# Transposes as pairs of 64-row tiles, narrower Gram products, SwiGLU on two slices at once, narrowing in four raw buffers, and a new instruction order

## The chip, the cores and the metric

The kernel runs on one core of one Trainium2 chip. The metric is the device time of one execution in microseconds (us); the time before is the median of three runs. One more execution was taken with the hardware profiler; its rows are the source of every duration in this document. Engines are called as in the profile: PE is the matrix engine (TensorE), PEld its weight loads, DVE the vector engine, ACT the scalar engine, POOL and SP the two engines that mostly issue transfers here.

## The reference

An RWKV-7 recurrence is followed by a SwiGLU feed-forward block. Shapes are batch 4, heads 8, sequence 768, head dimension 40; the outputs of the 8 heads side by side are the 320 features of 3072 tokens.

```python
for t in range(S):
    y[:, :, t] = np.einsum('bhd,bhde->bhe', rt, state)
    Sa = np.einsum('bhde,bhe->bhd', state, at)
    state_decay = state * wt[:, :, None, :] - np.einsum('bhd,bhe->bhde', Sa, bt)
    state = state_decay + np.einsum('bhd,bhe->bhde', vt, kt)
...
xn = x / rms * rms_g
g = xn @ w_gate
silu = g * (1.0 / (1.0 + np.exp(-g)))
val = xn @ w_val
return (silu * val @ w_out).astype(np.float32)
```

The weights `w_gate` and `w_val` are 320 x 1536 and `w_out` is 1536 x 320. They arrive as 64-bit floats: the kernel reads them as pairs of 32-bit words and makes 32-bit floats of them ("narrowing"). All matrix products are in 32-bit floats.

## The kernel before, in words

The sequence is cut into 24 chunks of 32 tokens; 32 sequences (batch x head) are worked on together. For a chunk, `front` loads the inputs token by token, turns them so that features lie on partitions, builds the decayed products of keys and values with the gates level by level (levels 1, 2, 4, 8, 16; these are the Gram products), and writes the triangular matrix LT of the chunk. `inverse` (for the first chunks `early_inverse`) inverts it on DVE. `main` makes the outputs of the chunk and the next state, turns the outputs back to tokens, normalizes them and turns them again into `xg`, the input of the feed-forward block. `front` runs two chunks ahead of `main`.

`feed` (L939) does the feed-forward block for a group of two chunks, 256 tokens. The 1536 hidden columns are 12 slices of 128, taken in six pairs. For each slice the weights (480 KB, one tile `wf`) are loaded from a copy `sW` in HBM; two products on 64 rows each (the last 64 features of gate and value; below "the 64-row products") and four on 128 rows give gate and value in PSUM, ACT makes `sg` = silu(gate), DVE makes `hT` = value * sg, and two products of 128 x 320 add the slice to the output `po`. Before group 0, and between its pairs, `narrow` (L973) makes the 24 halves of `sW` from the 64-bit weights, in the same rotating five `wf` tiles that `feed` uses.

A transpose on PE takes the data as the loaded operand and streams the identity through it. `turned` (L630) does eight of them, one for each pair of heads: the data of 128 rows is loaded with up to 104 columns, and 128 columns of identity are streamed; for K and ST it is 104 rows and 104 columns of identity. A chunk has such batches for wan, kbn, VU, K and ST, and one for rn in every second chunk; besides there are four transposes of y and three of x, 128 x 128 each. Transposes appear under L489, all products under L486.

A 32-bit product is two passes in the trace, so the profile counts two records for it; a transpose is one record. Small products use a part of the array each: the Gram products load 40 rows and 64 columns and stream 56 columns, so four of them have places of their own (two groups of rows, two of columns).

The order of all engines is written out. Each call of a helper adds a piece to `Plan`; `Plan.issue` takes the pieces in the order of the string `ORDER`, a number for each, and assigns one of three PSUM pairs ("rooms") by the string `PAIRS`. A "-" in `ORDER` puts a product of the identity with itself on PE (L1015, `plan.warm`), whose result is not used. Every engine works off its pieces in this order and waits at the first whose inputs are not there. `ORDER` has 6028 pieces and 151 of these warm products.

Of the kernel before, what the change touches and what calls it, by code (L numbers as in the profile page):

```python
# [17 lines left out]
P = 128  # L18
# [3 lines left out]
WB = 5  # L22
LEAD = 2
# [10 lines left out]
85 83 84 76 58 78 86 74 73 59 60 75 5 89 61 88 77 4 43 6 201 7 87 334 90 44 8 214 213 53 62 9 - - - - - - - - 93 18 10  # L34
567 335 557 11 12 13 79 14 15 94 566 80 210 16 95 558 108 17 200 - - - 97 96 19 20 100 21 2 22 101 23 98 25 568 202 24
26 107 112 57 - - - - - 102 106 111 124 27 209 122 392 103 109 52 119 113 104 54 578 569 577 155 199 125 110 105 204
120 - - - - - - 114 203 118 117 121 559 211 598 589 562 46 131 129 132 45 560 212 597 563 588 561 123 115 136 586 384
133 134 - - - - - 126 130 116 47 564 3 145 216 394 383 135 336 128 137 48 144 143 141 91 587 219 142 51 570 127 1005
565 146 138 337 55 573 579 281 393 220 582 608 571 390 234 239 607 572 583 580 380 574 251 222 38 221 609 575 581 42 -
- - - - - - - 223 82 226 339 64 379 227 338 39 81 139 224 263 149 576 238 153 56 249 247 590 206 584 228 382 237 591  # L40
593 272 40 233 232 381 154 0 593 32 139 390 204 228 591 388 234 249 247 - - 324 235 35 31 27 244 229 146 147 259 281
245 258 149 34 325 594 36 33 270 155 243 62 605 584 598 230 - 239 40 214 599 601 242 628 64 49 91 627 602 30 626 1135
600 28 48 257 603 29 241 68 150 255 65 0 1347 194 0 194 84 173 0 - - - 182 540 200 0 184 1 186 542 540 0 506 0 457 469
849 199 455 242 111 97 110 112 96 51 61 439 460 458 122 50 243 0 0 255 242 0 709 104 470 242 120 246 259 708 57 247
458 456 0 257 718 256 470 242 0 716 265 487 486 0 268 0 0 265 101 473 0 262 277 0 273 0 236 0 260 0 269 0 242 461 - -
- - - - - 237 0 240 0 278 242 252 0 242 252 0 90 0 0 98 99 246 0 0 230 440 0 230 94 93 457 440 231 - - - - - - - - -
240 441 244 0 44 0 468 440 255 0 450 468 269 469 0 257 214 439 238 213 203 0 257 203 93 449 92 0 0 234 - - - - - - - -
245 437 0 250 262 0 464 246 247 436 260 245 446 258 259 469 244 - - 255 471 465 468 470 466 0 269 215 255 478 466 93
94 264 95 96 266 97 0 97 470 1 2 98 99 0 0 96 467 97 469 98 468 251 265 99 470 100 471 101 441 102 103 258 104 105 260
106 - - - - - - - - - - - 0 106 107 471 108 0 108 502 503 472 0 108 109 110 111 0 0 0 0 0 - - 13 0 16 562 572 146 571  # L50
561 147 14 142 143 374 15 13 355 - - - 25 386 358 0 358 386 388 16 25 387 389 390 70 79 17 391 28 191 147 355 356 80
148 149 359 0 68 28 2 29 149 0 149 34 150 29 151 187 24 25 31 152 33 153 188 391 393 32 154 35 390 392 358 0 0 152 40
187 153 27 154 155 156 33 157 158 159 160 161 34 162 36 163 164 37 165 41 391 38 42 392 39 394 561 166 395 393 552 0
42 559 549 548 395 209 0 549 560 42 165 210 43 44 211 427 428 395 - - - 565 166 45 167 557 168 0 565 566 168 739 0 522
693 534 526 124 - - 0 526 124 139 0 535 681 682 579 0 535 545 547 140 536 138 141 0 547 545 555 543 578 0 558 520 567
- - - - - - 518 378 0 696 378 380 381 695 518 120 685 526 - - - - - - 522 686 379 527 382 136 530 383 554 529 121 - -
141 540 523 565 539 537 142 538 524 - - - - 145 525 148 534 149 152 154 551 535 147 555 - - 157 146 550 536 150 155
# [3 lines left out]
478 595 568 - - 35 830 594 567 820 38 36 - 476 37 571 366 570 0 605 356 433 434 435 436 120 437 0 317 318 319 320 441  # L61
321 322 323 355 456 324 458 459 442 4 357 325 457 326 327 443 328 0 443 328 329 330 331 357 0 35 0 330 2 37 450 359 3
36 358 331 332 357 333 356 0 462 330 461 464 448 331 332 468 364 447 463 31 467 476 458 333 365 334 335 0 425 439 441
302 426 436 0 6 439 2 0 435 332 2 436 443 444 0 448 332 442 334 443 333 340 449 0 32 297 329 342 330 - 3 338 33 341
334 0 332 331 0 332 293 441 0 438 0 436 293 333 336 295 337 309 438 338 1 375 342 310 365 374 515 27 292 0 362 26 28
44 339 29 34 292 27 32 338 0 646 29 34 336 32 0 439 64 315 647 646 339 440 441 63 340 0 287 413 312 313 623 12 414 314
415 315 416 608 624 32 417 480 418 625 419 420 421 316 626 638 33 0 312 417 625 418 - - - - 476 313 601 602 600 610
812 419 420 421 822 258 422 423 0 313 810 423 625 637 2 0 819 2 0 254 473 420 421 645 310 422 0 - - - - - 310 422 3
313 33 0 28 626 307 419 639 627 420 637 308 0 637 20 635 420 647 21 421 23 422 613 648 819 38 22 809 423 39 659 24 611
3 612 36 818 424 651 808 621 425 25 660 426 - 616 249 427 0 427 3 25 58 57 428 28 47 0 428 429 28 430 3 431 0 26 25  # L70
614 484 31 27 617 627 0 458 216 400 590 600 401 0 12 582 32 401 583 25 0 397 579 21 - - - - - - - - - 588 29 28 30 591
22 453 428 398 605 23 0 591 23 429 602 24 609 0 24 397 588 602 1 604 398 429 430 2 399 427 0 584 - - - - - - - - - - -
- - - 4 397 0 25 397 4 0 393 394 21 23 27 28 395 598 24 424 607 0 21 38 35 395 37 396 24 2 424 47 397 398 399 400 25
# [4 lines left out]
663 729 634 977 562 563 717 713 986 978 665 564 565 566 975 567 568 714 569 985 570 571 967 722 572 723 - 0 400 403  # L78
# [290 lines left out]
def kernel(  # L369
# [440 lines left out]
    def main(c):  # L810
# [29 lines left out]
        if c % 2 == 0:  # L840
# [8 lines left out]
            for i in range(2):  # L849
                (copy if c < LATE else dcopy)(R["r2"][half(i)], ps[half(1 - i), :, i])  # L850
# [80 lines left out]
        if c % CG == 0:  # L931
            xg[c // CG] = xg_.next()
# [115 lines left out]
```

## Time and profile before

| what | value |
|---|---|
| runs | 1063.64, 1070.07, 1071.96 us |
| median | 1070.07 us |
| span of the profiled execution, first to last instruction | 1060.6 us |
| device time of the profiled execution | not listed beside its span |
| PE busy | 1009.5 us, of which warm products 47.97 us |
| transposes on PE (L489) | 155.71 us |
| DVE busy | 842.3 us |
| ACT busy | 468.1 us |
| mean granted clock of PE | 0.979 |

The medians are times of the device for a whole execution; the span leaves out what lies before the first and after the last instruction. The listed runs are 3.0 to 11.4 us longer than the span, the median 9.5 us. A busy time is the union of the recorded intervals of a group, so groups that overlap on one engine add up to more than the engine's busy time. Intervals on PE overlap as well, because a pass begins before the end of the one before it; the pace of a batch is therefore read from the start of one batch to the start of the next, not from the duration of a pass.

### The profile page before, as it was taken

How to read it: one execution, taken by the hardware profiler on the slowest of the kernel's cores; microseconds unless marked ns; L12 is line 12 of the kernel's file. 1: busy time of each engine (PE TensorE's matmuls, PEld its weight loads, DVE VectorE, ACT ScalarE, POOL GpSimd, SP SyncE). 2: the span in 40 equal slices, each digit the busy share in tenths (PEclk: the TensorE clock that was granted, in tenths of full speed). 3: DMA queues.
4: the chain of work that ended last, by engine and by line, in shares of the span. 5: the costliest groups of instructions: out<-in, count | busy, mean ns of one | idle time of the engine just before them, and what ended most of it. 6: DMA issues, size and time to landing. Idle time of an engine off the chain costs nothing.

```text
span 1060.6 us, 53494 instructions
## 1 busy us (share of the span) xinstructions
PE 1009.5 (95%) x23406; PEld 829.3 (78%) x23406; DVE 842.3 (79%) x2861; ACT 468.1 (44%) x1043; POOL 309.5 (29%) x554
## 2 busy tenths in 40 slices
PE   7868999999999999999999999999999999999997
PEld 6767777777888778787778778787777888787875
DVE  8978878776868988898898798989889899787411
ACT  6856666643543534434443444434344443431211
POOL 8824413120532241241233241340331331110000
PEclk9777998999999999999999999999999999999999
DMA  9965458766565483655565555574555555443252
GB/s 168 216 155 133 77 127 207 211 123 178 127 140 126 106 173 96 150 134 125 123 155 129 135 132 114 122 160 119 137 126 126 138 137 138 100 132 102 80 162 68
DMA packets 172457, 143.35 MB, mean 135 GB/s; under 512 B 125504, under 2 KB 143872, under 8 KB 172224
## 3 DMA queue, kind: packets, MB, share of 16 engines
q1 hardware_dynamic: 153856, 116.96, 42.9%
q0 software_dynamic: 16192, 22.64, 12.1%
q8 instruction: 184, 3.01, 1.2%
q10 hardware_dynamic: 2176, 0.33, 0.3%
q14 instruction: 49, 0.40, 0.1%
HBM read 123.86 MB, written 15.99 MB: 132 GB/s over the span
## 4 chain that ended last, share of the span: by engine, by line
PE 72%; DVE 8%; DMA 4%; ACT 3%; issue 3%; POOL 2%; SPq 1%; DVEq 0%; ACTq 0%; POOLq 0%
PE ps L486 50%; PE po L486 13%; PE ps L489 8%; DMA wf<-sW 2%; DVE LT L444 1%; DVE y L444 1%; DVE tmp L444 1%; POOL kbn L483 1%; DVE Yi L444 1%; DVE K L444 1%; SPq L483 1%; DMA sY<-Yi 1%; ACT VU L467 1%; PE po L1015 0%; DVE Ab L444 0%
## 5 line engine op out<-in xcount | busy, mean ns | idle before, releaser
L486 PE MATMUL ps<-xg,wf 128*128 128x256 f32 (+1 forms) x1728 | 353.5, 390 | 4.0 <-DVE xg L444 2.0
L486 PEld LDWEIGHTS ps<-xg,wf 128*128 128x128 f32 (+1 forms) x1728 | 261.4, 188 | 57.2 <-issue 15.0
L486 PE MATMUL po<-wf,hT 128*128 128x320 f32 x576 | 183.1, 449 | 0.1
L464 ACT ACTIVATE sg<-ps 128x256 f32<-128x256 f32 x144 | 53.6, 382 | 228.2 <-PE ps L486 224.9
L444 DVE TENSOR_TENSOR tmp<-Yi,M 128x60 f32<-128x60 f32 (+24 forms) x620 | 130.7, 211 | 19.1 <-DMA M<-sB 5.9
L444 DVE TENSOR_TENSOR Yi<-Yi,tmp 128x60 f32<-128x60 f32 (+24 forms) x620 | 129.7, 209 | 12.7
L483 POOL DMA_DIRECT2D VU<-in_v_dram x92 | 53.2, 584 | 274.1 <-PE ps L486 141.8
L486 PEld LDWEIGHTS po<-wf,hT 128*128 128x128 f32 x576 | 102.5, 191 | 35.7 <-issue 4.1
L444 DVE TENSOR_TENSOR hT<-ps,sg 128x256 f32<-128x256 f32 x144 | 59.7, 420 | 67.2 <-ACT sg L464 66.4
L444 DVE TENSOR_TENSOR K<-K,T 128x512 f32<-128x512 f32 (+1 forms) x192 | 93.4, 496 | 8.3 <-PE ps L486 5.8
L486 PEld LDWEIGHTS ps<-Ab,K 40*64 40x64 f32 x4608 | 77.2, 138 | 28.1 <-issue 10.5
L467 ACT COPY K<-K 128x256 f32<-128x256 f32 (+1 forms) x168 | 71.7, 443 | 58.4 <-PE ps L486 39.2
L486 PE MATMUL ps<-Ab,K 40*64 40x56 f32 x4608 | 87.2, 224 | 9.7 <-issue 3.8
L444 DVE TENSOR_TENSOR As<-ps,msi 128x256 f32<-128x256 f32 (+1 forms) x186 | 78.9, 476 | 14.4 <-PE ps L486 13.8
L467 ACT COPY KN<-ps 128x640 f32<-128x640 f32 x96 | 66.1, 690 | 53.5 <-PE ps L489 23.3
L483 POOL DMA_DIRECT2D kbn<-in_b_dram x92 | 53.3, 583 | 96.7 <-PE ps L486 94.3
L486 PEld LDWEIGHTS ps<-As,KN 128*40 128x40 f32 x3072 | 66.5, 124 | 15.7 <-issue 10.4
L483 POOL DMA_DIRECT2D kbn<-in_k_dram x92 | 53.6, 585 | 82.7 <-PE ps L486 82.6
L486 PE MATMUL ps<-As,KN 128*40 128x32 f32 x3072 | 73.2, 205 | 3.1 <-issue 2.5
L483 POOL DMA_DIRECT2D wn<-in_w_dram x92 | 51.6, 567 | 62.7 <-DVE tmp L444 24.1
L444 DVE TENSOR_TENSOR y<-y,ps 128x256 f32<-128x256 f32 x119 | 50.0, 420 | 16.2 <-PE ps L486 13.7
L444 DVE COPY_PREDICATED LT<-near,ps 128x384 f32<-128x384 uint32 (+2 forms) x72 | 52.2, 725 | 2.6 <-PE ps L486 2.0
(133 smaller groups left out, 1546.0 us busy)
## 6 DMA issues: line engine op xcount, KB each, us to landing
wf<-sW SPq DMA_DIRECT2D x144, 480.0 KB, 3.9
M<-sB SPq DMA_DIRECT2D x80, 128.0 KB, 4.1
rn<-in_r_dram SPq DMA_DIRECT2D x24, 160.0 KB, 5.4
sW<-ex SPq DMA_DIRECT2D x16, 240.0 KB, 3.4
out_dram<-o SPq DMA_DIRECT2D x48, 80.0 KB, 4.2
kbn<-in_k_dram POOLq DMA_DIRECT2D x92, 40.0 KB, 3.9
kbn<-in_b_dram POOLq DMA_DIRECT2D x92, 40.0 KB, 4.1
wan<-in_a_dram POOLq DMA_DIRECT2D x46, 80.0 KB, 4.9
```

Of the source, the lines that this page charges most:

```text
L444: plan.add("DVE", kind, lambda at: fn(at(o), *m(at)), [o], aps(*args))
L464: plan.add("ACT", "act", lambda at: nc.scalar.activation(at(o), at(a), f, **kw), [o] + aps(acc), [a])
L467: plan.add("ACT", "copy", lambda at: nc.scalar.copy(at(o), at(a)), [o], [a])
L483: plan.add(by, "dma", lambda at: queue.dma_start(out=o, in_=i), [o], [i])
L486: return o, lhsT, rhs, lambda at: nc.tensor.matmul(at(o), lhsT, rhs, start=start, stop=stop, skip_group_check=True)
L489: return o, i, ident, lambda at: nc.tensor.transpose(at(o), i, ident)
```

## The change

- `turned` takes the data in two halves of 64 rows (`half`), or of 40 rows at partitions 0 and 64 (`part`, for K and ST), and makes sixteen transposes in place of eight. The halves lie in different groups of rows and write to different PSUM banks. The streamed identity has 64 columns (40 for K and ST) in place of 128 (104). The transposes of y become eight (40 rows, 40 columns), those of x six (64 rows, 64 columns). The tiles that receive them (vut, rE) have the two halves as an outer dimension. The copies of wan into A and Ab are two each in place of one.
- The Gram products of levels 4, 8 and 16 load 60, 56 and 48 columns in place of 64.
- In `feed`, one ACT instruction makes silu of both slices of a pair (512 columns), and one DVE instruction the product; the two output products of the pair come behind it. Before there was one of each for every slice (256 columns).
- `WB` is 6 in place of 5. Group 0 loads its slices into `wf` tiles 0 and 1 only; the other groups rotate over six. Narrowing uses tiles 0 and 1 for its first two halves, and then rotates over tiles 2 to 5; its third buffer `ex` is the tile of xg of the second group. All pieces of narrowing are added ahead of the chunks.
- `x` has one buffer in place of two, `tmp` is half as wide.
- `ORDER` and `PAIRS` are new: 5932 pieces and 175 warm products.

```diff
-WB = 5
-LEAD = 2
+WB = 6
...
-    def turned(t, at=lambda n: n, ins=P, outs=TOP):
-
-        ps = plan.room().rearrange("p u f -> p (u f)").rearrange("p (n t) -> p n t", n=N)
-        pe("turn", [flip(ps[0:outs, at(n), 0:ins], t[0:ins, n, 0:outs], ident[0:ins, 0:ins]) for n in range(N)])
+    def turned(t, at, outs=TOP, by=half, w=64):
+
+        ps = plan.room().rearrange("p u (n t) -> p u n t", n=N)
+        pe("turn", [flip(ps[0:outs, u, at(n), 0:w], t[by(u), n, 0:outs], ident[by(u), by(u)]) for n in range(N) for u in range(2)])
...
-        copy(A[:, :, :, 0:3], a4.rearrange("p n (g j) -> p n g j", j=4)[:, :, :, 1:4])
...
+        for i in range(2):
+            a4 = ps[:, i, :, C:]
+            copy(A[:, i::2, :, 0:3], a4.rearrange("p n (g j) -> p n g j", j=4)[:, :, :, 1:4])
...
-            pe("gramk", [mm(gr[half(i), o, n, 0:16 + D], K[part(o), 2 * n + i].rearrange("p x s -> p (x s)"),
+            pe("gramk", [mm(gr[i * 64:i * 64 + 64 - l, o, n, 0:16 + D], K[part(o), 2 * n + i].rearrange("p x s -> p (x s)")[:, 0:64 - l],
                             A[part(o), 2 * n + i, 16:]) for n, i, o in each])
...
-             turned(K.rearrange("p (n i) x s -> p n (i x s)", i=2), ins=TOP, outs=P).rearrange("p n (o e) -> p n o e", o=2)[:, :, :, 0:D])
+             turned(K.rearrange("p (n i) x s -> p n (i x s)", i=2), lambda n: n, P, part, D).rearrange("p o n e -> p n o e")[:, :, :, 0:D])
...
-        pe("turn4", [flip(xn[:, m], y.rearrange("p (m c) t -> p m (c t)", m=4)[:, m], ident) for m in range(4)])
...
+        pe("turn4", [flip(xv[:, o, m], yt[part(o), m], ident[part(o), part(o)]) for m in range(4) for o in range(2)])
...
-        pe("turn3", [flip(ps[:, kt, :], x[:, kt * P:(kt + 1) * P], ident) for kt in range(KT)])
+        ps = plan.room()[:, :, 0:KT * 64].rearrange("p u (k t) -> p u k t", k=KT)
+        pe("turn3", [flip(ps[:, u, kt], x[half(u), kt * P:(kt + 1) * P], ident[half(u), half(u)]) for kt in range(KT) for u in range(2)])
...
-                pe("h", [mm(h[e][:, q], wk[e][2 * q + kt], x[:, kt, :], False, kt == 1)
-                                           for q in range(2) for kt in range(2)])
-                act(sgs[:, e], h[e][:, 0], AF.Silu)
-                tt(hTs[:, e], h[e][:, 1], sgs[:, e], MUL)
-                pe("out", [mm(po[:, q, 0:DM], hTs[:, e, q * P:(q + 1) * P], wfs[e][:, 2 * P:2 * P + DM], f + e == 0, f + e == FT - 1)
-                                            for q in range(CG)])
+                pe("h", [mm(h[e][:, q], wk[e][2 * q + kt], x[:, kt, :], False, kt == 1) for q in range(2) for kt in range(2)])
+            act(sg, hh[:, 0], AF.Silu)
+            tt(hT, hh[:, 1], sg, MUL)
+            for e in range(2):
+                pe("out", [mm(po[:, q, 0:DM], hT[:, e * GT + q * P:e * GT + (q + 1) * P], wfs[e][:, 2 * P:2 * P + DM], f + e == 0, f + e == FT - 1)
+                           for q in range(CG)])
...
-        rw = wf_.next().bitcast(I32).rearrange("p (f w) -> p f w", w=2)[:, 0:n]
...
+    def wf_next(g, f):
+
+        return wf_.tiles[f % 2 if g == 0 else (g * FT + f) % WB]
...
+        rw = wf_.tiles[k if k < 2 else 2 + (k - 2) % 4].bitcast(I32).rearrange("p (f w) -> p f w", w=2)
```

More of the change, by code (lines that the diff above doesn't have):

```diff
@@ L278, in foot, with add @@
         return p, p + dims[0][1], self.masks[key]
-    def add(self, engine, kind, issue, outs, ins):
+    def add(self, engine, kind, issue, outs, ins, after=()):
         me = len(self.pieces)
@@ L320, in add @@
         self.pieces.append(piece)
+        return me
     def issue(self, order, pairs):
@@ L494, in issue @@
                 s[3](at)
-        plan.add("PE", kind, issue, [s[0] for s in steps] + more, [x for s in steps for x in s[1:3]])
+        return plan.add("PE", kind, issue, [s[0] for s in steps] + more, [x for s in steps for x in s[1:3]], after)
     ident = const.tile([P, P], FP32, name="ident")
@@ L532 @@
     eye = const.tile([P, C // 4, C], FP32, name="eye")
-    row, column, bits, same = (vut_.tiles[0][:, k, 0:C].bitcast(I32) for k in range(4))
+    row, column, bits, same = (vut_.tiles[0][:, 0, k, 0:C].bitcast(I32) for k in range(4))
     same = same.bitcast(FP32)
```

213 lines of the change are left out of this document (107 added, 106 removed), and 330 rows, old and new, of the table ORDER.

## The prediction

> **What bounds the kernel now.** I read the page first, then the busy times by stretch, then the groups by form for prices, then the timeline of PE for the pace of batches.
>
> ```profile
> span 1060.6 us, 53494 instructions
> PE 1009.5 (95%) x23406; PEld 829.3 (78%) x23406; DVE 842.3 (79%) x2861; ACT 468.1 (44%) x1043; POOL 309.5 (29%) x554
> ...
> PE 72%; DVE 8%; DMA 4%; ACT 3%; issue 3%; POOL 2%; SPq 1%; DVEq 0%; ACTq 0%; POOLq 0%
> ```
>
> PE is busy 95% of the span and holds 72% of the chain that ended last. By stretch (columns: stretch, then busy us of PE, PEld, DVE, ACT, POOL, the granted clock, DMA):
>
> ```profile
> 0.00:150.00 150.00, 124.46 (x3398) 109.78 (x3398) 125.16 (x381) 100.95 (x211) 76.28 (x155) 0.87 0.66 141
> 150.00:250.00 100.00, 95.84 (x2047) 77.89 (x2044) 75.23 (x257) 54.81 (x119) 25.05 (x43) 0.97 0.74 189
> 250.00:950.00 700.00, 684.26 (x16560) 559.23 (x16560) 599.20 (x2097) 290.74 (x662) 206.50 (x353) 1.00 0.55 131
> 950.00:1060.60 110.60, 104.97 (x1407) 82.42 (x1405) 42.67 (x129) 21.58 (x52) 1.68 (x3) 1.00 0.37 108
> ```
>
> ```profile
> 0.00:250.00 250.00, 47.97 (x302) 42.25 (x302) 0.91 0.69 160
> ```
>
> ```profile
> 0.00:150.00 150.00, 28.61 (x190) 22.71 (x190) 0.87 0.66 141
> 150.00:1060.60 910.60, 127.10 (x1026) 108.17 (x1026) 1.00 0.55 134
> ```
>
> The second fence is the warm products alone (L1015), the third the transposes alone (L489). Three stages follow. Up to 150 us DVE is the fuller engine, 125.16 against PE's 124.46, of which most of the 47.97 us of warm products must still come off. From 250 to 950 us PE has 15.7 us of idle time in 700, so what PE saves there is time saved, as long as DVE (599.2, 85.6%) keeps up. At the end only `feed` is left and PE alone decides. I count PE savings behind 150 us, 127.10/155.71 = 82% of them, that is 24 x 0.82 = 19.6 chunks, and at nothing before, where DVE, ACT and the transfers for narrowing cover PE.
>
> **Transposes.** The pace of a batch is the distance to the start of the next (start us, duration, ...):
>
> ```profile
> 705.16 0.92 PE L489 MATMUL ps<-ident,ST 104*104 104x104 f32 x8
> 705.92 0.60 PE L489 MATMUL ps<-ident,y 128*128 128x128 f32 x4
> 706.36 0.88 PE L489 MATMUL ps<-ident,K 104*128 104x104 f32 x8
> 707.07 1.26 PE L486 MATMUL po<-wf,hT 128*128 128x320 f32 x4
> 708.17 1.04 PE L489 MATMUL ps<-ident,rn 128*104 128x128 f32 x8
> 709.04 1.04 PE L489 MATMUL ps<-ident,wan 128*104 128x128 f32 x8
> 709.92 0.49 PE L489 MATMUL ps<-ident,x 128*128 128x128 f32 x3
> 710.25 0.97 PE L486 MATMUL po<-wf,hT 128*128 128x320 f32 x3
> ```
>
> ST takes 0.76 us, y 0.44, K 0.71, rn 0.87, wan 0.88, x 0.33. The time follows the streamed columns: 128 take 110 ns, 104 take 89 to 95. Taking kbn and VU like wan, a chunk has 3.5 x 0.88 + 0.71 + 0.76 + 0.44 + 0.33 = 5.32 us.
>
> Two transposes on separate groups of 64 rows are not in the trace; the nearest rows are the 64-row products of `feed`, which load 128 columns and run in pairs:
>
> ```profile
> 1013.85 0.73 PEld L486 LDWEIGHTS ps<-xg,wf 64*128 64x128 f32 x8 [0.44 <-DVE xg L444]
> 1014.91 1.59 PEld L486 LDWEIGHTS ps<-xg,wf 128*128 128x128 f32 x8 [0.33 <-issue]
> 1016.84 0.73 PEld L486 LDWEIGHTS ps<-xg,wf 64*128 64x128 f32 x8 [0.33 <-issue]
> ```
>
> Four pairs of 256 columns take 1.06 us, 265 ns a pair, 1.035 ns for a column; a pair of 64 columns is 66 ns, one of 40 is 41. The other limit is the load. For it I use the Gram products, next to a product with the same load and fewer streamed columns:
>
> ```profile
> L486 PE MATMUL ps<-Ab,K 40*64 40x56 f32 x4608 | 87.2, 224 | 9.7 <-issue 3.8 <-DVE K L444 1.8 <-ACT KN L467 1.7
> L486 PE MATMUL ps<-rE,vut 40*64 40x32 f32 x1536 | 27.6, 220 | 1.2 <-ACT vut L467 0.6 <-issue 0.3 <-ACT KN L467 0.2
> ```
>
> ```profile
> 600.48 1.16 PE L486 MATMUL ps<-Ab,K 40*64 40x56 f32 x64 [0.18 <-DVE LT L444]
> 601.57 0.62 PE L486 MATMUL ps<-VU,LT 32*32 32x40 f32 x46
> ```
>
> 56 streamed columns take 87.2/4608 = 18.9 ns and 32 take 27.6/1536 = 18.0, so the load of 64 columns sets the pace there. A batch of 64 records takes 1.09 us, four records 68 ns, in which each group of rows loads twice 64 columns: at most 0.53 ns for a column if a group loads one after another. 104 columns are then 55 ns, 128 are 68. I take the larger of load and stream, the loads of the two groups side by side as in these rows: 66 ns for wan, kbn, VU, rn; 68 for K, y and x; 55 for ST. A chunk becomes 3.5 x 0.53 + 0.54 + 0.44 + 4 x 0.068 + 3 x 0.068 = 3.31 us, 2.01 less; 19.6 chunks give **-39.4 us**.
>
> The trace of before bounds the price of a load from above as well: K loads 128 columns in a pace of 0.71/8 = 89 ns, at most 0.69 ns a column. [...]
>
> **Gram products.** Four, eight and sixteen columns fewer, twice per group of rows, are 4.2, 8.5 and 17 ns of 68, but 56 streamed columns at 0.86 ns (110/128) keep 48 ns: 16 x (4 + 8 + 17) = 0.46 us a chunk, 9 us counted; nothing if the load isn't what binds. I take half, **-4.7 us**.
>
> **Changes between array divisions.** Turn batches move from undivided rows to halves.
>
> ```profile
> 691.38 1.04 PE L489 MATMUL ps<-ident,VU 128*104 128x128 f32 x8
> 692.35 0.92 PE L486 MATMUL ps<-xg,wf 64*128 64x256 f32 x6
> ```
>
> In front of a 64-row product the batch takes 0.97 us in place of 0.88, so a change costs 0.09. PE's instruction order has 375 such changes before and 469 after, counting the 64-row products with their group: 94 x 0.09 x 0.82 = **+7 us**.
>
> **SwiGLU, copies, DVE, ACT.**
>
> ```profile
> L444 DVE TENSOR_TENSOR hT<-ps,sg 128x256 f32<-128x256 f32 x144 | 59.7, 420 | 67.2 <-ACT sg L464 66.4
> L464 ACT ACTIVATE sg<-ps 128x256 f32<-128x256 f32 x144 | 53.6, 382 | 228.2 <-PE ps L486 224.9 <-DVE Yi L444 2.4 <-DVE hT L444 0.5
> L444 DVE TENSOR_TENSOR As<-ps,msi 128x512 f32<-128x512 f32 x42 | 28.4, 683 | 9.6 <-PE ps L486 9.6
> L467 ACT COPY T<-ps 128x512 f32<-128x512 f32 x24 | 14.1, 588 | 14.2 <-PE ps L489 10.0 <-DVE tmp L444 4.2
> L467 ACT COPY Ab<-ps 128x128 f32<-128x128 f32 x24 | 9.6, 400 | 4.7 <-PE ps L489 4.7
> ```
>
> 72 products of 512 columns like As, 683 ns, replace 144 of 420: 49.2 against 59.7 us, DVE -10.5. ACT goes from 53.6 to 72 x 0.588 = 42.3, and gets 48 more copies of at most 0.4 us, 19 us at most against 11.3 saved; ACT is busy 44% of the span, which hides it. Queued behind a later hT on DVE are its other pieces, behind the later silu ACT's copies. The first silu of a pair now waits for the second slice's products, and a room is held 0.588 + 0.683 - 0.382 - 0.420 = 0.47 us longer per pair; other products fill PE meanwhile. Without that cover it costs 72 x 0.47 = 34 us. On the path for certain it lies once, behind the last pair: **+0.5 us**.
>
> **Narrowing, group 0, order.**
>
> ```profile
> 137.72 0.42 DVE L444 TENSOR_TENSOR hT<-ps,sg 128x256 f32<-128x256 f32 x1 [0.52 <-ACT sg L464]
> ...
> 231.99 0.42 DVE L444 TENSOR_TENSOR hT<-ps,sg 128x256 f32<-128x256 f32 x1
> ```
>
> ```profile
> wf<-sW SPq DMA_DIRECT2D x144, 480.0 KB, 3.9
> ```
>
> Group 0 runs from 138 to 232 us by its first and twelfth hT. With two `wf` tiles, the loads of a pair must wait for the outputs of the pair before: 3.9 (landing) + 1.06 + 2 x 1.93 (the h rows above) + 0.59 + 0.68 + 2 x 1.10 = 12.3 us a pair, 74 for six. The 94 us cover it; SP queues behind each waiting load the loads of narrowing. The narrowing pieces themselves are as many as before, on SP, ACT and DVE. Adding the means of DVE's rows along its new order, the work ahead of group 0's last hT falls by about 9 us; narrowing and transfers also bind there, so I take half, **-5 us**, between 0 and -9. Warm products rise from 302 to 350 records, 7.6 us at 47.97/302, where PE waits anyway: 0. Six `wf` tiles in the later groups let a third pair load early: 0, a small gain not excluded.
>
> With 34 us less, the stage of 700 us has 591 of DVE in 666, 89%. That has been reached with PE nearly full:
>
> ```profile
> 850.00:900.00 50.00, 49.34 (x1123) 41.02 (x1122) 46.38 (x166) 20.18 (x44) 13.69 (x24) 1.00 0.54 134
> ```
>
> DVE 93%, PE 99%. I add **+3 us** of waits (between 0 and 16, a doubling of PE's idle time).
>
> **Sum.** 1060.6 - 39.4 - 4.7 + 7 + 0.5 - 5 + 3 = 1022.0 us of span. The time of the profiled execution isn't listed beside its span; the median lies 9.5 us above the span, which I keep: 1031.5.
>
> **The rivals.**
> *Dearer loads, side by side.* At K's bound of 0.69 ns a column 104 columns are 72 ns and 128 are 89: a chunk's transposes 3.5 x 0.58 + 0.71 + 0.58 + 0.36 + 0.27 = 3.95, -26.8 us, and the Grams then bind on the stream: 1060.6 - 26.8 + 7 - 5 + 3 + 0.5 + 9.5 = 1048.8. For it: x and y with 128 columns are no faster than the stream. Against: with 104 streamed columns K, which loads 128, is no slower than ST, which loads 104. [...]
> *Loads of a pair one after another (slower).* Place: each of the sixteen transposes. Price: 55 to 72 ns for 104 columns, 68 to 89 for 128, sixteenfold, eightfold for y, sixfold for x: 6.0 to 7.8 us a chunk, +13 to +49 us; with the Grams' 4.7 at the cheap end, the other terms and 9.5 the time is 1084 to 1125, in the middle 1104. It decides as soon as a pair of 64 columns takes more than 110 ns, the pace of one present transpose. Against it: four loads in 68 ns are too many for one after another at 0.53.
> *DVE becomes the bound.* If its 85.6% in the middle stage is already its limit, only its own saving counts, 10.5/0.856 = 12.3 us: 1060.6 - 12.3 + 9.5 = 1057.8. For it: DVE is the second engine; against: the stretch at 93%.
> *Group 0 stretches.* If a pair's loads and products, with other work between, take 18 us for 12.3, group 0 takes 108 for 94, +14: 1045.5.
> *The rooms take it back.* The 34 us of longer holding in full: 1065.5, no change that can be told.
>
> **How the numbers follow.** Chances: the forecast 0.45; dearer loads 0.12 (the page's rule goes with it); loads in turn 0.08; DVE 0.15; group 0 0.10; rooms 0.10. The forecast's own range is 1010 to 1046 (Grams 0 to -9, start 0 to -9, waits 0 to 16, streams at 0.86 ns). A measurement of this kernel tells about 1% from no change, 1059.4 to 1080.8. Faster: 0.45 + 0.12 + 0.10 and half of DVE's, 0.75; same: the other half and 0.08 of the rooms, with 0.01 of loads in turn, 0.16; slower: 0.07 and 0.02, 0.09. The range 1005 to 1062 leaves out the loads in turn, most of the rooms and a little below.
>
> **What would show it.** In the changed profile the turn batches should start the next batch after 0.5 us, and L489's 155.7 us fall by a third or more; L486's Ab,K rows should fall under 18.9 ns a record for the narrower loads; PE should be busy over 96% between 250 us and the end, and DVE about 89%. Turn batches at 0.8 us or more would make the main term wrong; PE idle above 35 us in that stage would mean DVE or the rooms; a first hT later than 138 us, or group 0 longer than 94 us, the start.

## The result, and the profile after

The changed kernel takes 1172.47 us (median of 4 runs, 1168.09 to 1176.45), the kernel before, on the same chip, 1068.58 us. The ratio is 1.0989, with a 95% interval of 1.0938 to 1.104: the change makes the kernel 10% slower. The prediction said 1031.5 us and gave "slower" 9 in 100. One of the four runs of e21 (below) was slow, 1104.9 us; the figures given here leave it out, while the expectations recorded after it use the median of all four, 1088 us.

The page of the changed kernel: span, busy times, chain, and queue q8, which the page calls "instruction".

```profile
span 1174.7 us, 55743 instructions
PE 1033.2 (88%) x24670; PEld 829.5 (71%) x24670; DVE 834.7 (71%) x2789; ACT 451.8 (38%) x1019; POOL 312.9 (27%) x554
...
q8 instruction: 194, 3.18, 1.2%
...
PE 59%; DVE 15%; DMA 12%; issue 8%; ACT 3%; SPq 2%; POOL 1%; DVEq 0%; ACTq 0%
```

No engine became the bound: PE fell from 95% to 88%, DVE from 79% to 71%. In the chain PE lost 13 points; DVE gained 7, transfers (DMA) 8, and "issue", time in which an engine waited for nothing that the profile shows, 5. By stretch, and then the transposes alone:

```profile
0.00:150.00 150.00, 117.63 (x3180) 106.07 (x3180) 108.46 (x325) 91.21 (x197) 76.06 (x153) 0.81 0.66 143
...
250.00:950.00 700.00, 628.10 (x15430) 498.02 (x15433) 530.33 (x1823) 254.87 (x592) 185.82 (x314) 0.92 0.50 116
```

```profile
0.00:150.00 150.00, 17.76 (x348) 13.88 (x348) 0.81 0.66 143
150.00:1174.00 1024.00, 90.09 (x2084) 75.30 (x2084) 0.92 0.49 119
```

The transposes did what was forecast: 107.85 us in place of 155.71, although the clock was lower. But from 250 to 950 us PE stood 71.9 us where it had stood 15.7, at a granted clock of 0.92 where it had been 1.00. PE's waits, before and then after (us in total, times, longest):

```profile
PE ps L486 <- issue: 16.9, 25, 1.8
```

```profile
PE ps L519 <- issue: 58.4, 37, 4.5
PE ps L519 <- DMA LT<-sY: 13.3, 4, 4.9
PE ps L519 <- DMA wf<-sW: 11.0, 5, 3.6
PE ps L522 <- issue: 7.1, 4, 5.0
```

One such wait on the timeline, in the middle of a batch of 64 equal products, with the stretches before and behind it (the clock is the third figure from the right):

```profile
560.46 1.12 PE L519 MATMUL ps<-As,KN 128*40 128x32 f32 x49
565.86 0.74 PE L519 MATMUL ps<-As,KN 128*40 128x32 f32 x15 [4.28 <-issue]
566.54 1.07 PE L522 MATMUL ps<-ident,K 40*128 40x40 f32 x16
567.41 4.89 PE L519 MATMUL ps<-xg,wf 64*128 64x256 f32 x16
572.23 0.66 PE L522 MATMUL ps<-ident,wan 64*104 64x64 f32 x16
572.82 0.78 PE L519 MATMUL ps<-ST,aP 40*32 40x40 f32 x64
```

```profile
550.50:561.50 11.00, 10.84 (x256) 8.62 (x255) 9.70 (x39) 3.05 (x7) 0.56 (x1) 1.00 0.60 155
566.00:572.00 6.00, 6.00 (x47) 4.58 (x47) 4.25 (x18) 0.69 (x1) 2.30 (x4) 0.56 0.61 149
```

After 49 of 64 products PE stands 4.28 us with all its data there, and then runs 6 us at about half clock: sixteen 64-row records of 256 columns take 4.89 us, where eight had taken 1.06 us in the trace of before. At full clock again, the pairs of wan take 0.59 us (572.23 to 572.82); the forecast was 0.53. Half clock can be added up from the mean clock, since the clock records of both traces hold only 1.0 and 0.5: before (1 - 0.979) x 1060.6 / 0.5 = 45 us, after (1 - 0.909) x 1174.7 / 0.5 = 214 us. Work at half clock takes about twice as long (the sixteen records above, 4.89 us for 2 x 1.06), so about half of the extra 170 us is lost time, an estimated 85 us. That is why PE's busy time rose by 24 us (11 of them warm products) with 48 us less of transposes. The time in which PE stood rose by 90 us, from 51.1 to 141.5 (span less busy time); the two rises are the 114 us by which the span grew.

What arrives at the end of such a gap can be seen in the transfers: q8 made 194 transfers of 16 KB for 24670 records of PE, 184 for 23406 before: about 127 records, each a load and a product, to a transfer. The closest two of the 194 start 3.38 us apart. Of the 42 waits marked "issue", 40 end 1.2 to 1.6 us after such a transfer has ended. The first theory was therefore **instruction supply**: pairs and clustered small products use up instructions faster than they come. Its rival was that the **new order** is at fault.

### The profile page after: what moved, and what is told of

It reads as the page before. It is cut to its first block, busy times and chain, and to the rows that moved or that the text cites. A ratio compares the mean times of both kernels' runs of the same rounds, so it can differ in the third digit from the quotient of the medians.

```text
span 1174.7 us, 55743 instructions
## 1 busy us (share of the span) xinstructions
PE 1033.2 (88%) x24670; PEld 829.5 (71%) x24670; DVE 834.7 (71%) x2789; ACT 451.8 (38%) x1019; POOL 312.9 (27%) x554
## 4 chain that ended last, share of the span: by engine, by line
PE 59%; DVE 15%; DMA 12%; issue 8%; ACT 3%; SPq 2%; POOL 1%; DVEq 0%; ACTq 0%
PE ps L519 42%; PE po L519 11%; PE ps L522 4%; DMA wf<-sW 4%; DVE tmp L477 3%; DMA LT<-sY 3%; DVE Yi L477 2%; SPq L516 2%; DMA sY<-Yi 1%; DVE LT L477 1%; DVE As L477 1%; PE po L1048 1%; DVE K L477 1%; DMA sB<-LT 1%; DVE y L477 1%
## 5 line engine op out<-in xcount | busy, mean ns | idle before, releaser
L519 PE MATMUL ps<-xg,wf 128*128 128x256 f32 (+1 forms) x1728 | 394.3, 429 | 20.4 <-DMA wf<-sW 11.0
L519 PEld LDWEIGHTS ps<-xg,wf 128*128 128x128 f32 (+1 forms) x1728 | 286.5, 210 | 85.6 <-issue 31.8
L519 PEld LDWEIGHTS po<-wf,hT 128*128 128x128 f32 x576 | 107.2, 196 | 40.9 <-issue 4.8
L497 ACT ACTIVATE sg<-ps 128x512 f32<-128x512 f32 x72 | 43.0, 598 | 206.9 <-PE ps L519 206.7
L477 DVE TENSOR_TENSOR hT<-ps,sg 128x512 f32<-128x512 f32 x72 | 49.5, 687 | 78.7 <-ACT sg L497 78.5
L519 PE MATMUL ps<-Ab,K 40*60 40x56 f32 (+2 forms) x4608 | 83.7, 223 | 20.8 <-issue 11.2
L519 PEld LDWEIGHTS ps<-Ab,K 40*60 40x60 f32 (+2 forms) x4608 | 73.4, 134 | 33.6 <-issue 18.4
L477 DVE TENSOR_TENSOR As<-ps,msi 128x256 f32<-128x256 f32 (+1 forms) x186 | 82.6, 478 | 10.2 <-ACT As L503 7.5
L516 POOL DMA_DIRECT2D VU<-in_v_dram x92 | 55.6, 605 | 125.8 <-PE ps L519 81.7
L1048 PE MATMUL po<-ident 128*128 128x128 f32 x350 | 59.1, 322 | 3.8 <-POOL VU L512 3.3
```

What stands on the lines that cost most here:

```text
L477: plan.add("DVE", kind, lambda at: fn(at(o), *m(at)), [o], aps(*args))
L497: plan.add("ACT", "act", lambda at: nc.scalar.activation(at(o), at(a), f, **kw), [o] + aps(acc), [a])
L516: plan.add(by, "dma", lambda at: queue.dma_start(out=o, in_=i), [o], [i])
L519: return o, lhsT, rhs, lambda at: nc.tensor.matmul(at(o), lhsT, rhs, start=start, stop=stop, skip_group_check=True)
L1048: plan.warm = lambda: nc.tensor.matmul(po_[:, 0, DM:DM + P], ident, ident, start=False, stop=False, skip_group_check=True)
```

## Experiments

Each row is the median, its ratio to the kernel before in runs on the same chip, and the 95% interval. "Rows" are transposes of full rows as before; "short loads" bring only an eighth of the bytes of `wf` from the third group on, so these kernels (e21 to e24) leave out most of the weights in those groups and don't compute the block's result.

| kernel | us | ratio |
|---|---|---|
| old order, pairs alone (e1) | 1117.31 | 1.0495 (1.0458 to 1.0532) |
| old order, narrower Gram loads alone (e2) | 1062.46 | 0.9972 (0.9945 to 0.9999) |
| new order, all but the pairs (e3) | 1153.94 | 1.0835 (1.0802 to 1.0868) |
| old order, everything (e7) | 1173.94 | 1.1061 (1.0988 to 1.1134) |
| old order, all but the pairs (e8) | 1148.85 | 1.0785 (1.0714 to 1.0856) |
| old order, Gram and new buffers (e10) | 1082.03 | 1.014 (1.0089 to 1.0192) |
| old order, Gram and SwiGLU of two (e11) | 1135.80 | 1.0668 (1.0596 to 1.074) |
| e11, two instructions at the common place (e15) | 1129.84 | 1.0594 (1.0535 to 1.0654) |
| changed kernel, output products spread (e13) | 1209.29 | 1.1371 (1.1276 to 1.1465) |
| e2, output products spread (e14) | 1082.29 | 1.0145 (1.0068 to 1.0223) |
| old order, pairs of 64 columns only (e16) | 1090.16 | 1.027 (1.0219 to 1.0322) |
| before, copies of A and Ab in two (e17) | 1063.61 | 1.0002 (0.9978 to 1.0027) |
| changed kernel, small loads first (e20) | 1160.87 | 1.0913 (1.0845 to 1.0982) |
| changed kernel, short loads (e21) | 1084.99 | 1.022 (1.0167 to 1.0273) |
| before, short loads (e22) | 1051.46 | 0.9868 (0.9812 to 0.9925) |
| e1, short loads (e23) | 1084.72 | 1.0186 (1.0109 to 1.0263) |
| e11, short loads (e24) | 1116.25 | 1.0486 (1.0415 to 1.0556) |

### One part at a time in the old order

**Pairs alone.** Into the kernel before go only the new `turned`, `turn4` and `turn3` with their copies.

> The kernel before with its own order of pieces, in which only the transposes are made as pairs of 64-row tiles (turn, turn4, turn3). Theory 1 (instruction supply): the second half of the pairs is twice the instructions in half the time, PE runs dry in runs of small products and then falls to half clock; transposes fall from 155.7 to about 108 us, but PE's idle time put down to issue rises from 17 us to over 30, the mean clock falls under 0.97, and the time is 1045 to 1100. Theory 2 (the new order is at fault): the old order keeps PE full, the mean clock stays at 0.98, and the time is the predicted gain without the SwiGLU change, 1022 to 1040.

It took 1117.31 us. The rival's figure is refuted, and the loss is larger than the theory's range, which ended at 1100: the pairs cost 5% under the order that had been fitted to the old transposes.

```profile
span 1115.2 us, 56003 instructions
PE 1021.2 (92%) x24622; PEld 817.3 (73%) x24622; DVE 841.8 (75%) x2861; ACT 467.7 (42%) x1091; POOL 310.0 (28%) x554
```

```profile
PE ps L492 <- issue: 41.5, 40, 3.3
PE ps L495 <- issue: 5.3, 4, 2.4
```

PE's waits for instructions went from 16.9 to 46.8 us, the mean clock to 0.934, an estimated 147 us at half clock if its clock too was only 1.0 or 0.5. No wait for a transfer of data is among the larger ones.

**Narrower Gram loads alone.** Into the kernel before goes only the narrower load of the Gram products.

```diff
-            pe("gramk", [mm(gr[half(i), o, n, 0:16 + D], K[part(o), 2 * n + i].rearrange("p x s -> p (x s)"),
+            pe("gramk", [mm(gr[i * 64:i * 64 + 64 - l, o, n, 0:16 + D], K[part(o), 2 * n + i].rearrange("p x s -> p (x s)")[:, 0:64 - l],
...
```

> The kernel before with its own order, in which only the Gram products of levels 4, 8 and 16 load 60, 56 and 48 columns. Both theories: as many instructions as before, so no new gaps; the rows of the narrower products fall from 18.9 ns a record to 18.7, 18.0 and 18.0 as in the changed kernel; the time is 1060 to 1070, a gain of at most 9 us.

It gains 0.28%, 3 us, within what was expected; its interval just excludes no gain. Of the kernels here that compute the whole result it is the fastest, and it holds the only part of the change that paid.

**Where the pairs' cost sits.** Two further kernels: one with pairs only for wan, kbn, VU, rn and x, and one that splits only the two copies on ACT (A, and Ab alike).

```diff
-copy(A[:, :, :, 0:3], a4.rearrange("p n (g j) -> p n g j", j=4)[:, :, :, 1:4])
+copy2([(A[:, i::2, :, 0:3], a4[:, i::2].rearrange("p n (g j) -> p n g j", j=4)[:, :, :, 1:4]) for i in range(2)])
```

> The kernel before with pairs only where 64 rows of a half are turned (the batches wan, kbn, VU, rn and x); K, ST and y keep full rows. All pairs in this order took 1117 us. Theory 'instruction supply': of some 1,200 extra records some 750 are left, the saving of these batches is the larger one (0.35 us a batch), so about half of the loss is left: 1080 to 1105 us. Rival 'pairs of 40 rows': they alone cost (two records of 52 ns for one of 90 to 110), 1030 to 1068 us. Rival 'copies and row groups': the loss is as before, 1108 to 1125 us.

> The kernel before, with only the two copies of A and Ab on ACT split into two instructions each (48 more instructions on ACT), which the pairs brought along. Theory 'instruction supply': ACT is busy 44%, 1062 to 1076 us. Rival 'copies': they delay the Gram products of every chunk and make up a large part of the 50 us, 1085 to 1115 us.

The copies cost nothing that can be told (1.0002). The pairs of 64 columns cost 2.7% with 744 extra records (24150 against 23406), all pairs 5.0% with 1216: the loss goes about with the number of added instructions, and not with one kind of pair. Waits for instructions were 32.1 us (28.4 and 3.7). The changes between array divisions, which the prediction put at 7 us, grow with the pairs as well; no run tells them apart.

**The supply by itself.** A kernel with nothing but a stream of products and transposes on PE, no waits between them, its outputs zeros. Every kind comes twice. 60 loads of 1.3 MB run beside the first round until 240 us, so that its last products, those on 32 x 32, come without loads already.

> PE alone, without the computation (the output is zeros): 512 transposes of 128 rows, 1024 of 64 rows in pairs (64 columns), 1024 of 40 rows in pairs (40 columns), 768 Gram-like products, 768 products of 32 by 32, each run between large products, and all of it twice, the first time beside 60 loads of 1.3 MB. Theory 1: the large and the 128-row products keep an even pace of 110 ns a transpose; the others start at their own pace and then break into bursts with gaps put down to issue, 256 instructions per 3.4 us or more, that is 27 ns a record or more on the mean, where alone they would need 33, 21 to 34, 17 and 11. Theory 2: even paces of 33, 34, 17 and 11 ns a record, without gaps.

Pairs of 64 columns beside the loads, products on 32 x 32 without them, the pairs of 64 columns again without loads, and pairs of 40 without loads:

```profile
129.06 3.78 PE L79 MATMUL ps<-ident,data 64*104 64x64 f32 x128 [2.41 <-issue]
135.26 3.78 PE L79 MATMUL ps<-ident,data 64*104 64x64 f32 x128 [2.41 <-issue]
...
307.75 1.64 PE L67 MATMUL ps<-data 32*32 32x40 f32 x128 [2.10 <-issue]
311.48 1.64 PE L67 MATMUL ps<-data 32*32 32x40 f32 x128 [2.09 <-issue]
...
434.58 26.37 PE L79 MATMUL ps<-ident,data 64*104 64x64 f32 x927
461.17 2.94 PE L79 MATMUL ps<-ident,data 64*104 64x64 f32 x97 [0.23 <-issue]
...
478.05 51.97 PE L83 MATMUL ps<-ident,data 40*128 40x40 f32 x1024
```

In the pairs beside the loads and in the products on 32 x 32, 128 records stand between one gap marked "issue" and the next. With idle transfer engines (2% busy) 128 of the products on 32 x 32 come about every 3.7 us (3.5 to 4.0), 29 ns a record, about what the pairs use without gaps (28.4 ns a record: 26.37 us / 927). With busy ones (93%) 128 records of the pairs come every 6.2 us (5.4 to 6.7), 48 ns a record, and a pair then costs 97 ns for the 110 of a full transpose (56.06 us / 512). So fewer records come while large loads are under way. Even then a pair of 64 columns is no dearer than the transpose that it replaces. What it changes is how fast instructions are used: two records in 57 ns, where the old transpose was one in 110. In the kernel with pairs alone 41.5 of the 46.8 us of waits for instructions stand at products, not at transposes. That fits pairs that leave too few instructions for the small products around them, but no run shows this step by itself.

The pairs of 40 columns, which load 128, missed the expectation: they kept an even 51 ns a record without loads, where 21 to 34 were expected, so a pair takes 101 ns in so long a run; beside the loads it was 54 ns, at a granted clock of 0.50 (167.20 to 210.10 us). In the changed kernel's short batches they are faster: the four pairs of y at 576.17 us take 0.27 us.

By stretch: pairs beside the loads (transfer engines 93% busy), the products on 32 x 32 (PE busy 43%, clock 0.57), and pairs without loads:

```profile
100.30:144.30 44.00, 31.31 (x1025) 30.42 (x1024) 0.00 (x0) 0.00 (x0) 0.96 0.93 352
...
292.10:335.40 43.30, 18.57 (x1537) 16.79 (x1536) 0.00 (x0) 0.00 (x0) 0.57 0.02 4
434.60:464.10 29.50, 29.27 (x1026) 28.94 (x1025) 0.00 (x0) 0.00 (x0) 1.00 0.02 4
```

The gaps of 2.1 to 2.7 us in the products on 32 x 32, one in every 3.7 to 4.0 us, stand beside a granted clock of 0.57. In the changed kernel 22 gaps exceeded 2 us, before 3; for 17 of the 22 a stretch at half clock begins 1.1 to 4.0 us after the gap's start, and 2 more gaps begin inside one.

### Order against parts

**The new order with rows.** The changed kernel, transposes undone inside their pieces, order kept (`turned`; those of y and x alike).

```diff
...
-pe("turn", [flip(ps[0:outs, u, at(n), 0:w], t[by(u), n, 0:outs], ident[by(u), by(u)]) for n in range(N) for u in range(2)])
...
+pe("turn", [flip(ps[0:outs, at(n), 0:ins], t[0:ins, n, 0:outs], ident[0:ins, 0:ins]) for n in range(N)])
```

> The changed kernel with its new order, in which only the transposes are again 8, 4 and 3 of 128 (104) rows. PE gets 48 us of transposes back. Theory 1 (instruction supply): the idle time put down to issue falls to under half of the 60 us that the changed kernel has, the mean clock rises from 0.909 to 0.95 or more, and the time falls to 1110 to 1150 although PE has more to do. Theory 2 (order): the waits stay where they are, the clock stays at 0.90 to 0.92, and the time is 1172 to 1215.

It took 1153.94 us, just above the first theory's range and far below the second's. The clock rose to 0.948, close to what was expected, but the waits for instructions fell only to 49.8 us (44.2 at products, 5.6 at transposes), not to under 30. The pairs cost 1.4% in the new order (1.0989 / 1.0835), and 8.4% stayed. I took these to be the new order's own, and tested it by giving the changed kernel's pieces the old order.

> All parts of the change (pairs, narrower Gram loads, SwiGLU of two slices, four raw buffers, six wf tiles), but the pieces are issued in the order of the kernel before; 73 of 6,000 pieces, which the new buffers would not let go at their old place, go as soon as they can. Theory 'two costs': pairs cost what they cost in the old order alone (1117 us), and what is left of the loss, some 55 us, is the new order itself, so this kernel takes 1100 to 1135 us. Rival 'parts': SwiGLU of two slices with its longer held rooms, the two wf tiles of group 0 and the raw buffers are what costs the rest, in any order: 1145 to 1185 us, near the changed kernel's 1172.

> As the kernel with all parts in the old order, but with transposes of full rows again: so only narrower Gram loads, SwiGLU of two slices, raw buffers and wf tiles are new. Theory 'two costs': without pairs and without the new order nothing of the loss is left, 1050 to 1080 us, about the kernel before. Rival 'parts': 1115 to 1155 us, near the 1154 of full rows in the new order. Under 1055 us the parts beside pairs and order would be a gain.

My theory fell: both came out at the rival's figures (1173.94 and 1148.85). All of the change costs the same in either order, so the order was not what made it slow. The waits differ, though: with rows in the old order PE waited for `hT` and ACT, in the new order for instructions (44.2 us) and for LT (13.3).

**Which part.** First silu and product slice by slice with the new buffers (its code is compared with that of e8, all but the pairs), then the reverse.

```diff
-            act(sg, hh[:, 0], AF.Silu)
-            tt(hT, hh[:, 1], sg, MUL)
+                act(sg[:, s], h[e][:, 0], AF.Silu)
+                tt(hT[:, s], h[e][:, 1], sg[:, s], MUL)
```

> Order of the kernel before, transposes of full rows, narrower Gram loads, the new buffers (raw words in four of six wf tiles, group 0 with two), but silu and product again slice by slice at their old places. Its neighbour, the same kernel with SwiGLU of two slices, took 1149 us; narrower Gram loads alone 1062. Theory 'SwiGLU of two': the second slice's products, one silu and one product of 512 now stand in one chain on which ACT, DVE and PE wait in turn, and that costs some 55 us or more of the 80: 1062 to 1095 us here. Rival 'buffers': two wf tiles in group 0 and the raw tiles cost the larger part: 1115 to 1150 us.

> The counterpart: order and buffers of the kernel before, full rows, narrower Gram loads, and SwiGLU of two slices alone (79 of 6,000 pieces later than in the old order, most of them the first slice's output products, which have to wait for the common product). Theory 'SwiGLU of two': 1105 to 1150 us. Rival 'buffers': 1055 to 1085 us. Both between 1090 and 1110 would mean that the two share the cost.

SwiGLU of two slices costs 7% by itself (1.0668 / 0.9972), the new buffers 1.7% (1.014 / 0.9972). DVE between 320 and 950 us, first in the kernel before, then with SwiGLU of two (e11); and PE's wait in e11 over the whole span:

```profile
DVE hT L444 <- ACT sg L464: 10.0, 14, 1.3
```

```profile
DVE hT L455 <- ACT sg L475: 27.3, 13, 4.9
```

```profile
PE po L497 <- DVE hT L455: 14.6, 22, 1.5
```

Slice by slice, PE computes the second slice while ACT and DVE finish the first, and DVE stands at most 1.3 us at a product. With two at once, DVE stands up to 4.9 us, and what is behind it on its queue can't start. Against e2, which differs by this part and the pieces moved for it alone, PE's waits for DVE rise from 18.7 to 46.3 us and those for ACT from 9.2 to 26.9. Only 14.6 us of them are at the output products that need `hT`; the others are spread over the pieces of the chunks. For a room that `hT` must leave first, PE waits 1.2 us in all, as before (1.0), so the longer held rooms are not the cost. The last test of this part keeps the common place, but puts two instructions of 256 columns there (silu; the product alike).

```diff
-            act(sgs.rearrange("p e t -> p (e t)"), hh[:, 0], AF.Silu)
...
+                for e in range(2):
+                    nc.scalar.activation(at(sgs[:, e]), at(h[e][:, 0]), AF.Silu)
...
```

> As the kernel with SwiGLU of two slices alone (1136 us), but at the common place stand two silus and two products of 256 columns each, one behind the other. Theory 'the place': that the first slice waits for the second, and everything on ACT and DVE behind it, is what costs: 1115 to 1155 us. Rival 'the size': that one instruction of 512 columns spans both slices is what costs, and separate ones let the first half start in time: 1055 to 1090 us.

1129.84 us, with an interval that overlaps that of the single instruction: it is the place that costs, not the size of the instruction.

### Transfers

**Spreading.** If clusters of small products are what starves PE, large ones should be put between them. Output products were moved later in `ORDER` into runs of small ones, nothing else.

> The changed kernel with 104 of its 144 output products (4 records of 320 columns each) issued a little later, into runs of small products: runs of 128 and more records between two large products fall from 92 to 63. Nothing else moves. Theory 'instruction supply' (PE eats records of small products faster than its instructions arrive, stands, and then runs at half clock): the gaps marked issue fall from 58 us to under 45 and half clock with them, 1130 to 1162 us for 1172. Rival: the output products hold wf and hT longer, the loads behind them on SP come later still, 1165 to 1200 us.

> The kernel before with narrower Gram loads (1062 us) and 94 of its 144 output products moved in the same way: runs of 128 and more records fall from 83 to 69. Theory 'instruction supply': a few us of the 19 us of gaps marked issue go, 1052 to 1062 us. Rival: the output products are late for the next loads and products, 1063 to 1085 us.

Both got slower, as the rival said, the changed kernel even by more (1209.29 us, where the rival ended at 1200). In the changed kernel the waits for instructions did fall, and others took their place:

```profile
PE ps L519 <- issue: 38.3, 30, 3.1
PE ps L519 <- DMA LT<-sY: 23.0, 7, 5.9
PE ps L519 <- DMA wf<-sW: 20.2, 5, 8.4
```

An output product sets when its `wf` tile comes free, so SP stood 301.8 us for output products in place of 219.5, and the loads of `wf`, and LT behind them on the same queue, came later. Moved like this, the order had no slack to give. The next two kernels take the transfers themselves: 12 loads of `wf` behind the small loads of LT and M that follow them, and then the `wf` loads cut short.

```diff
+            some = slice(0, P if g < 2 else 16)
             for e, wf in enumerate(wfs):
-                dma(wf, sW[f + e])
+                dma(wf[some], sW[f + e][some])
```

> The changed kernel, with 12 of its 132 loads of wf (480 KB) put behind the small loads of LT and M that directly follow them on SP, 1 to 4 places later. Theory 'wf ahead of LT': the 13 us in which PE waits for LT go, and the half clock behind them, 1145 to 1166 us for 1172. Rival: these waits only move to wf or to the instructions, 1166 to 1185 us.

> The changed kernel, but the loads of wf from the third group on bring only 16 of 128 rows, an eighth of the bytes (what the other rows hold is left over from the second group, so the result is not the reference's); every wait of SP, PE and the order stay. If the bytes on the transfer queues are a main cause of the loss, some 31 us of waits and the half clock behind them go: 1110 to 1150 us. If they only come on top of what PE would wait for anyway: 1155 to 1180 us.

Small loads first: 1160.87 us, ratio 1.0913; the waits for LT halved (6.5 us) and the median lies in the theory's range, but the interval overlaps that of the changed kernel, so this one is unclear. Short loads: 1084.99 us, better than any expectation. With an eighth of the bytes the loss falls from 9.9% to 2.2%. Its stretch from 250 to 950 us, its waits of PE, and its short loads of `wf` (median time to landing last; the long ones of the changed kernel took 5.1 us):

```profile
250.00:950.00 700.00, 666.00 (x17245) 531.62 (x17245) 590.86 (x2038) 282.47 (x657) 208.72 (x354) 0.97 0.36 71
```

```profile
PE ps L519 <- issue: 31.3, 23, 3.7
PE ps L519 <- DMA LT<-sY: 7.2, 7, 3.3
```

```profile
wf<-sW SPq DMA_DIRECT2D x120, 60.0 KB, 3.0
```

Not only the waits for data fall, but those for instructions too, from 58.4 to 31.3 us, with the same instructions in the same order. The controls apply the same cut to the kernel before and to the two costly parts.

> The kernel before with loads of wf cut to 16 of 128 rows from the third group on (the other rows are left over, so the result is not the reference's): the control for the changed kernel with the same cut, which fell from 1172 to 1088 us. Theory 'instructions behind bytes': this kernel loses only 15 us to missing instructions and none to late transfers, so it gains little: 1042 to 1063 us. Rival: shorter loads help any kernel alike, 7%: 985 to 1010 us.

> Pairs alone in the old order (1117 us), with the same cut of the wf loads (its result is not the reference's). Theory 'instructions behind bytes': the extra instructions of the pairs come late because they share the transfer engines with the wf loads, so most of the 52 us goes: 1040 to 1080 us. Rival 'instruction rate alone': 128 records in 3.5 us is the limit with or without other transfers, 1090 to 1120 us.

> SwiGLU of two slices alone in the old order with narrower Gram loads (1136 us), with the same cut of the wf loads (its result is not the reference's). Theory 'the place': DVE and ACT stand at the common silu and product, no transfer is part of it, 1105 to 1137 us. Rival 'transfers': pairs of wf loads let go together and the transfers behind them are what costs, 1045 to 1085 us.

PE's waits with short loads, pairs alone and then SwiGLU of two:

```profile
PE ps L492 <- issue: 23.4, 27, 2.3
```

```profile
PE po L497 <- DVE hT L455: 15.6, 22, 1.5
```

The cut is worth 1.3% to the kernel before, so it is not a gift to any kernel. Against that control (0.9868) pairs alone cost 3.2% in place of 5.0%, just outside the expected range and a third less, not most of it (PE's waits for instructions at products fell from 41.5 to 23.4 us), SwiGLU of two with the Gram loads 6.3% in place of 6.7%, and the changed kernel 3.6% in place of 9.9%. So a third of the pairs' cost goes with the bytes, through instructions that come sooner; the place of SwiGLU costs with or without them. The changed kernel then costs less than its two dear parts multiplied (9.7%). Whether the new order absorbs them once the transfers are short, or the parts overlap so in any order, is not shown: all parts in the old order were not run with short loads.

## Why the prediction was wrong, step by step

- **Transposes, -39.4 us: the size was right, the step to the path was not.** Busy time fell by 47.9 us over the span, 37.0 of them behind 150 us (127.10 to 90.09), where the prediction counted them. The sentence that failed is "what PE saves there is time saved, as long as DVE (599.2, 85.6%) keeps up". It knew two limits of a transpose, load and stream, and not the third, its instructions: the half-size transposes add 1216 records to 23406, and in e4 128 records came about every 3.7 us, every 6.2 us beside large loads. The pairs with their 1216 more records gave +5.0% by themselves in place of a gain: PE's waits for instructions rose by 30 us, and its time at half clock by an estimated 100.
- **Clock: costed at nothing.** The rows of the prediction hold granted clocks of 0.87 and 0.97 in the two early stretches, and it drew nothing from them. In the changed kernel 214 us ran at half clock, before 45; by the estimate above that is 85 us of lost time.
- **SwiGLU of two, +0.5 us: the largest wrong term in the old order,** where it cost 7%, 73 us. The prediction named the right place ("queued behind a later hT on DVE are its other pieces") and gave it a cover ("other products fill PE meanwhile") that the trace had not shown. Its price for the uncovered case, 34 us, was half of what came, and for another place: it counted how long a room is held, for which PE waited 1.2 us in all, while PE's waits for DVE and ACT rose by 45 us.
- **Narrowing and group 0, -5 us:** the buffers cost about 1.7%, 18 us, in the old order. The stretch of group 0 was right: 158 to 250 us after, 92 us for 94. But it starts 20 us later, a sign of being wrong that the prediction named. Two `wf` tiles in group 0, six later and the raw tiles were not told apart.
- **Gram products, -4.7 us:** -3 us measured (interval -6 to 0); right.
- **Changes between array divisions, +7 us:** not measured by itself.
- **Waits of the new order, +3 us:** wrong. From 250 to 950 us PE stood 56 us more. The prediction looked at DVE for them; they came from transfers and instructions. Its sign "PE idle above 35 us in that stage would mean DVE or the rooms" came, with 71.9 us, and meant neither.
- **DVE at 89%:** it stood at 76% (530.33 of 700). Its own saving came as forecast (`hT` 59.7 us before, 49.5 after), but nothing ran fast enough to need it. The rival that DVE becomes the bound was wrong as well.

No rival held the mechanism. "Rooms" stood near the place of SwiGLU, with a cost that didn't come; "loads in turn" had the right sign for a wrong reason, since a pair of 64 columns takes 57 ns and not over 110 (e4). "Dearer loads" fell by the same figure: two loads of 104 columns side by side fit into 57 ns, where it had 72. A rule for loads, which the chances count with it, is shown by no run; what the traces show are these 57 ns and the 89 ns of K, which loads 128 columns.

The parts measured one by one in the old order multiply to 1.0495 x 1.0668 x 1.017 = 1.139, all together gave 1.1061: they overlap. The new order by itself can't be told from the old one (1.0989 and 1.1061, intervals overlap). Open stays what SwiGLU of two costs in the new order alone, and how much of the loss is half clock and how much the gaps before it, since only the estimate above parts them. Full rows, one slice at a time and the narrower Gram loads in an order made for them would be the version to try; here it exists only as the kernel with narrower Gram loads in the old order, 0.28% under the kernel before.

## What to carry to other kernels

Cutting the 128-row transpose in two took PE from 110 to 57 ns and from one record to two: before counting busy time as saved, count instructions against their supply (here 128 products with their loads about every 3.7 us beside idle transfer engines, every 6.2 us beside busy ones) over the densest stretches, and count the large transfers that run beside them. Merging two steps of a pipeline saved instructions here and cost overlap, 7% of the time: the price was not on the engine that executes the merged one, but on what is queued behind it while it waits for its later half. And on an engine that had been 95% busy, gaps of over 2 us were, by the estimate above, dearer than they look, because a stretch at half clock began at most of them (17 of 22).

## What the runs showed of the hardware

- Queue q8 moved 16 KB in each transfer, one for about 127 load-and-product records of PE (194 for 24670 in the changed kernel, 184 for 23406 before). In e4, 128 records came about every 3.7 us with the transfer engines 2% busy, every 6.2 us beside loads that kept them 93% busy.
- Two 64-row transposes side by side take 57 ns on PE (28.4 ns a record), where one of 128 rows takes 110 (both in e4).
- In e4, products on 32 x 32 with gaps of 2.1 to 2.7 us every 3.7 to 4.0 us ran at a granted clock of 0.57. In the changed kernel's trace 31 of its 33 stretches at half clock last 3.41, 6.83 or 10.24 us.
